# A gated block without Strassen: split operands and three single-pass products, attention first

## The chip, the core and the metric

The kernel runs on one core of a Trainium2 chip. The core has five engines with instruction queues of their own: TensorE (matmuls; PE in the profile, its weight loads PEld), VectorE (DVE), ScalarE (ACT), GpSimd (POOL) and SyncE (SP). Here POOL and SP mostly issue DMA transfers. Matmul results go to PSUM, eight banks of 128 partitions x 512 float32. The metric is the device time of one execution, in microseconds (us); lower is better.

## The reference

Two blocks, one after the other. The attention has 4 batches of 8 heads, 768 tokens and 64 dimensions; a token sees only tokens whose 6-bit hash equals its own. The gated block maps 3072 tokens of 512 values through two weight matrices of 512 x 1536, a silu and a third matrix.

```python
q_bits = (np.einsum('bhsd,dk->bhsk', q, proj) > 0)      # the same for k; 6 bits make a bucket
mask = q_bucket[:, :, :, None] == k_bucket[:, :, None, :]
scores = np.where(mask, scale * np.matmul(q, k.transpose(0, 1, 3, 2)), -1e9)
attn = np.exp(scores - scores.max(-1, keepdims=True))
attn_out = np.matmul(attn / attn.sum(-1, keepdims=True), v)
x = attn_out.transpose(0, 2, 1, 3).reshape(B * S, H * D)
g = x @ w_gate
out = (g * (1 / (1 + np.exp(-g))) * (x @ w_val)) @ w_out
```

The weights arrive as 64-bit floats, so the kernel has to make 32-bit ones of them itself.

## The kernel before

**Attention.** The work goes by pairs of heads, 4 pairs for each of the 4 batches, 16 in all. A pair has two halves (384 query tokens), a half has six units (128 key tokens). `score` (L484) makes the scores of a unit: one float32 matmul per head, and one bf16 matmul on the hash bits that pushes unequal buckets far down; ScalarE takes the exponential into a tile `A`. `attend` (L500) multiplies by v into a bank that collects six units. `add` (L518) sums the exponentials over the units on VectorE, one operation of 128x768 a unit. `total` (L529) sums over partitions with a matmul by ones and takes a reciprocal on VectorE (L548, 384 columns wide); `norm` (L558) applies it. `front` (L388) prepares the next pair: for the first pairs TensorE transposes q and k, and from pair 5 on VectorE does (L457, two operations a pair); then hash matmuls (L412), signs on ScalarE (L417), and spreading of the bits (L426 on VectorE, L429 as a DMA on SP's queue).

**Weights.** `prepare` (L354) is a generator whose steps are handed out along the program. `narrow` (L304) makes float32 of a piece of 128x512 with two ScalarE operations (L297, L298) and three VectorE ones (L311, L313, L316). `form` (L329) makes the sums that the Strassen form needs, and stores blocks in DRAM (`ram`), from where `bring` (L322) fetches them again for each batch with POOL's queue into `room`.

**Gated block.** All products are float32 matmuls, issued at L593 by `product`. `up_strassen` (L599) computes both up products of a batch with seven half-size products in place of eight (Strassen, Winograd's form), and in batches 1 to 3 two of the seven are split once more in the same way (`deeper`, L703, 192 columns). `down_strassen` (L763) does the same with the down product (256 columns). The additions of the form run on VectorE (`plus`, L596), the gate is a tanh on ScalarE (L570) and two VectorE operations.

**Order.** The order of the instructions on each engine is that of the Python text. The main loop (L862) goes over half-pairs. The gated block of a batch is cut into atoms, and once the first batch's attention is done (from half-pair 9 on, `LATE`, L478), each turn issues one half-pair of attention and then atoms up to a credit. So attention of one batch and gated block of the batch before stand side by side through most of the span.

## Time and profile before

| | |
|---|---|
| time, median of 3 runs | 985.93 us (985.88 to 986.16) |
| span of the profiled execution | 983.9 us |
| profiled execution, with the 2.0 us around its span (taken from the median) | 985.9 us |
| TensorE busy | 977.7 us, 4813 matmul records |
| VectorE busy | 669.6 us |
| ScalarE busy | 408.2 us |
| GpSimd busy | 127.2 us |
| moved by DMA | 107.02 MB, mean 109 GB/s |

The span runs from the first to the last instruction. A program's float32 matmul leaves two matmul records, each with a weight load. A record is longer than the time until the next record starts, since matmuls are pipelined; the pace is read from start to start. In the list of groups a line gives: line of the program, engine, operation, output tile <- input tiles, shape, type and count, then busy time and mean ns, then the idle time before with what ended it. In the timeline a line begins with the start and the length of a run of like instructions. `q0` in the DMA table is POOL's queue, with packets, MB, and the time of its packets as a share of 16 DMA engines' span.

### The profile page before, as it was taken

The numbers are of one execution on the slowest core, as the hardware profiler recorded it, in microseconds if no ns is written. First come the engines' busy times: TensorE is split into PE (matmuls) and PEld (weight loads), VectorE is DVE, ScalarE is ACT, GpSimd is POOL, SyncE is SP. The second block draws the span as 40 slices with busy tenths as digits, with TensorE's granted clock in tenths as the row PEclk, the third lists the DMA queues.
The fourth block names the chain that finished last, engine by engine and source line by source line (L and its number), as shares of the span: only waits on it lengthen the run. The fifth ranks groups of instructions, "written<-read, shape, count | busy, mean of one in ns | idle before, by whom it ended". The sixth has DMA issues, their size and how long they took to land.

```text
span 983.9 us, 13575 instructions
## 1 busy us (share of the span) xinstructions
PE 977.7 (99%) x4813; PEld 624.2 (63%) x4813; DVE 669.6 (68%) x1276; ACT 408.2 (41%) x921; POOL 127.2 (13%) x248
## 2 busy tenths in 40 slices
PE   9999999999999999999999999999999999999998
PEld 4444555555576776556567776666556687666787
DVE  5899888888974647768775465676767444767721
ACT  6999555566413225444342224335443212333200
POOL 3232232241100011101110001110101000121000
PEclk9999999999999999999999999999999999999999
DMA  7787685976303043323432204343122011333000
GB/s 231 219 259 220 153 260 171 242 271 172 110 17 78 17 100 106 86 85 93 109 93 45 66 17 113 93 98 103 58 67 76 22 38 65 107 102 110 18 28 33
DMA packets 119987, 107.02 MB, mean 109 GB/s; under 512 B 90032, under 2 KB 104848, under 8 KB 119920
## 3 DMA queue, kind: packets, MB, share of 16 engines
q0 software_dynamic: 18336, 73.29, 23.0%
q1 hardware_dynamic: 100784, 32.67, 14.2%
q8 instruction: 38, 0.62, 0.3%
q10 hardware_dynamic: 800, 0.20, 0.1%
q14 instruction: 29, 0.24, 0.1%
HBM read 81.79 MB, written 17.30 MB: 101 GB/s over the span
## 4 chain that ended last, share of the span: by engine, by line
PE 95%; DVE 2%; ACT 2%; issue 1%; DVEq 0%; ACTq 0%
PE up L593 42%; PE po L593 22%; PE sc L494 15%; PE av L509 12%; PE sum L540 1%; PE hps L412 1%; PE tps L396 1%; ACT A L497 1%; ACT kb L417 1%; DVE room L368 0%; PE idle L134 0%; DVE acc L527 0%; ACT room L497 0%; DVE hid L575 0%; DVE c L571 0%
## 5 line engine op out<-in xcount | busy, mean ns | idle before, releaser
L593 PE MATMUL up<-xT,room 128*128 128x384 f32 (+1 forms) x732 | 243.0, 465 | 0.0
L593 PEld LDWEIGHTS up<-xT,room 128*128 128x128 f32 x732 | 134.8, 190 | 73.3 <-issue 9.8
L593 PE MATMUL up<-xc,room 128*128 128x384 f32 (+1 forms) x540 | 176.9, 455 | 0.0
L327 POOL DMA_DIRECT2D room<-ram x144 | 77.6, 542 | 671.0 <-PE up L593 654.3
L494 PE MATMUL sc<-qT,kT 64*128 64x384 f32 x768 | 159.5, 493 | 0.0
L527 DVE TENSOR_TENSOR acc<-acc,A 128x768 f32<-128x768 f32 x128 | 122.6, 958 | 15.7 <-ACT A L497 2.9
L597 DVE TENSOR_TENSOR c<-c,up 128x192 f32<-128x192 f32 (+1 forms) x198 | 78.8, 406 | 76.7 <-PE up L593 72.3
L593 PEld LDWEIGHTS up<-xc,room 128*128 128x128 f32 x540 | 99.3, 190 | 43.8 <-DVE c L597 1.1
L570 ACT ACTIVATE th<-c 128x384 f32<-128x384 f32 x90 | 47.0, 522 | 156.4 <-DVE c L571 87.6
L497 ACT ACTIVATE A<-sc 128x384 f32<-128x384 f32 x256 | 104.0, 527 | 0.6 <-PE sc L494 0.5
L815 ACT COPY words<-po 128x256 f32<-128x256 f32 x48 | 17.9, 372 | 198.5 <-PE po L593 179.6
L494 PEld LDWEIGHTS sc<-qT,kT 64*128 64x128 f32 x768 | 66.1, 186 | 53.6 <-issue 41.2
L597 DVE TENSOR_TENSOR hid<-hid,up 128x192 f32<-128x192 f32 (+1 forms) x162 | 67.6, 418 | 42.8 <-PE up L593 41.0
L509 PE MATMUL av<-A,vraw 128*64 128x384 f32 (+1 forms) x512 | 88.2, 486 | 0.0
L597 DVE TENSOR_TENSOR words<-words,po 128x256 f32<-128x256 f32 x36 | 15.1, 420 | 95.8 <-PE po L593 95.8
L679 ACT COPY c<-up 128x384 f32<-128x384 f32 x72 | 34.4, 478 | 81.6 <-PE up L593 81.6
L593 PE MATMUL po<-wo,room 128*128 128x256 f32 x288 | 66.3, 379 | 0.5 <-DVE room L597 0.5
L593 PE MATMUL po<-wo,hid 128*128 128x256 f32 x288 | 66.7, 382 | 0.0
L593 PE MATMUL po<-room,hid 128*128 128x256 f32 x288 | 66.2, 379 | 0.5 <-ACT words L815 0.5
L509 PEld LDWEIGHTS av<-A,vraw 128*64 128x64 f32 x512 | 36.7, 137 | 46.0 <-issue 44.4
L494 PE MATMUL sc<-qb,kb 64*128 64x384 bf16 x384 | 63.2, 323 | 0.5 <-DVE kb L426 0.5
L593 PEld LDWEIGHTS po<-wo,hid 128*128 128x128 f32 x288 | 54.1, 190 | 12.1 <-issue 4.9
(137 smaller groups left out, 1166.1 us busy)
## 6 DMA issues: line engine op xcount, KB each, us to landing
room<-ram POOLq DMA_DIRECT2D x96, 384.0 KB, 3.7
vraw<-in_v_dram SPq DMA_DIRECT2D x16, 384.0 KB, 3.3
ram<-room POOLq DMA_DIRECT2D x12, 512.0 KB, 5.0
room<-ram POOLq DMA_DIRECT2D x48, 128.0 KB, 3.5
out_dram<-words SPq DMA_DIRECT2D x48, 128.0 KB, 1.7
room<-in_moe_w_out_dram POOLq DMA_DIRECT2D x10, 512.0 KB, 6.6
qraw<-in_q_dram SPq DMA_DIRECT2D x48, 96.0 KB, 3.0
hid<-in_moe_w_gate_dram POOLq DMA_DIRECT2D x9, 512.0 KB, 6.9
```

The lines of the kernel that those rows point to most:

```text
L327: nc.gpsimd.dma_start(places[k % 2][:, PARTS[go], :], ram[k % NG][:, PARTS[go], :])
L396: nc.tensor.transpose(ps[:, i * P : (i + 1) * P], raws[name, n][:, half * CH + i, :, :].rearrange("p h d -> p (h d)"), ident)
L412: nc.tensor.matmul(tile_[i * BLOCK : (i + 1) * BLOCK, 0:HQ], hash_w, T[name, n][:, half * HQ : (half + 1) * HQ], start=True, stop=True)
L494: nc.tensor.matmul(sc[h], x["k", n][rows, ks], x["q", n][rows, qs], start=start, stop=not start)
L497: nc.scalar.activation(weights(u)[:, h, 0:HQ], sc[h], AF.Exp, scale=SCALE * (OFF / 2 if n <= NP else 1.0))
L509: nc.tensor.matmul(ps[h * D : (h + 1) * D, 0:width], raws["v", n][:, h, c, :], a[:, h, 0:width], start=c == 0, stop=c == NCH - 1)
L527: nc.vector.tensor_tensor(acc[n, half], acc[n, half], a[:, :, 0:HQ], op=ALU.add)
L570: nc.scalar.activation(th, g, AF.Tanh, scale=0.5)
L593: nc.tensor.matmul(ps, a, x, start=start and i == 0, stop=i == len(pairs_) - 1, skip_group_check=True)
L597: nc.vector.tensor_tensor(o, a, b, op=op)
L679: nc.scalar.copy(tile_of(g, spot), c)
L815: nc.scalar.copy(o, c)
```

## The change

Nearly the whole program is rewritten, though attention keeps its instructions.

- All 16 pairs of attention come first, then the gated blocks of all four batches. Nothing of the gated block stands beside attention, apart from weight preparation (four steps a half-pair, until 25 of 36 pieces are stored; the rest one step an atom in the first gated blocks).
- The operands of the gated block are split in a high and a low part, both rounded to the short float32r type, and the difference of the two. Each product is made of three float32r matmuls: high by high and low by low into one bank, difference by difference into another; 4097 times the first less the second is the product. There is no Strassen form.
- x is split after `norm` (a ScalarE cast and two VectorE operations), stored in DRAM (1.2 MB a pair), and loaded back per batch. A weight piece gets a cast on ScalarE and two VectorE operations beyond the three of before, and is stored with its three parts (786 KB). For every use a tile of a ring of seven is loaded with POOL's queue: 144 loads in the gated blocks.
- The reciprocal of the sums works on 12 columns: the sums are laid out by a DMA over 128 partitions, inverted, and spread again through DRAM.
- The exponential tiles form a ring of eight in place of six. The gate is ScalarE's Silu.

The core of the diff; what is left out of attention is moved and indented, not changed:

```diff
-    def narrow(i):
-        ...
-        nc.vector.tensor_tensor(wi, wi, lo, op=ALU.add)
-    def form(n):
-        ...
+    def prepare():
+        for i in range(NPIECE):
+            load_words(i + 1)
+            if i not in staged:
+                scale(i)
+            ...
+            nc.vector.tensor_tensor(wi, wi, lo, op=ALU.add)
+            nc.scalar.activation(r32(st[:, 0]), w, AF.Copy, scale=TOWARD)
+            load_words(i + 4)
+            yield True
+            nc.vector.tensor_tensor(r32(w), w, st[:, 0], op=ALU.subtract)
+            yield True
+            nc.vector.scalar_tensor_tensor(out=r32(st[:, 2]), in0=w, scalar=-STEP, in1=st[:, 0],
+                                           op0=ALU.mult, op1=ALU.add)
+            nc.gpsimd.dma_start(ram[i].bitcast(FP32), st)
+            progress["kept"] = i + 1
+            yield True
+    def bring(count=1):
+        for _ in range(count):
+            ...
+            while progress["kept"] <= at:
+                next(preparing)
+            held[what, n] = t = ringp.tile([P, 3, PIECE], FP32R, tag="ring", name="ring")
+            nc.gpsimd.dma_start(t.bitcast(FP32), ram[at].bitcast(FP32))
         def total(n):
             ...
-            nc.vector.reciprocal(r, ps[:, 0:HQ])
+            nc.scalar.copy(row, ps[:, 0:HQ])
+            few = att.tile([P, each], FP32, tag="few", name="few")
+            nc.sync.dma_start(few, row.rearrange("(g r) t -> r g t", r=BLOCK)[0])
+            waiting.append(lambda: invert(n, few))
+        def invert(n, few):
+            nc.vector.reciprocal(few, few)
+            nc.sync.dma_start(s, few)
+            ...
+            for h in range(2):
+                nc.sync.dma_start(t[h * D : (h + 1) * D].rearrange("p x t -> p (x t)"),
+                                  flat[h : h + 1].to_broadcast([D, 2 * HQ]))
+            return lambda: norm(n, t)
         def norm(n, t):
             nc.vector.scalar_tensor_tensor(out=x, in0=x, scalar=mean[n], ...)
+            nc.scalar.activation(h, x, AF.Copy, scale=TOWARD / STEP)
+            nc.vector.scalar_tensor_tensor(out=l, in0=h.bitcast(FP32), scalar=-STEP, in1=x,
+                                           op0=ALU.mult, op1=ALU.add)
+            nc.vector.tensor_tensor(d, h.bitcast(FP32), l.bitcast(FP32), op=ALU.subtract)
+            nc.sync.dma_start(kept_x[pairs[n]].bitcast(FP32), p.bitcast(FP32))
-    def up_strassen(x, b, first):
-        ...
-    def down_strassen(out_of, at_once):
-        ...
+    def gated_block(scope):
+        ...
+        pp = scope.enter_context(tc.tile_pool(name="pp", bufs=4, space=PSUM))
+            def first():
+                for half in halves_():
+                    for j in range(NJ):
+                        for v in range(2):
+                            mm(a[:, half, 0:HQ], block(v, j), xparts[b, j][:, v, halves[half]],
+                               j == 0 and v == 0, j == NJ - 1 and v == 1)
+            def second():
+                for half in halves_():
+                    for j in range(NJ):
+                        mm(n_[:, half, 0:HQ], block(2, j), xparts[b, j][:, 2, halves[half]],
+                           j == 0, j == NJ - 1)
+                    def one(what=what, z=z):
+                        ops[what] = up(n, what)
+                        ops[what][0]()
+                        nc.scalar.activation(two(z), ops[what][2], AF.Copy, scale=STEP + 1)
+                    def other(what=what, z=z):
+                        _, second, _, n_ = ops[what]
+                        second()
+                        bring()
+                        nc.vector.tensor_tensor(two(z), two(z), n_, op=ALU.subtract)
+                        if what == "g":
+                            nc.scalar.activation(z, z, AF.Silu)
+                            return
+                        nc.vector.tensor_tensor(val, gate, val, op=ALU.mult)
+                        nc.scalar.activation(h, val, AF.Copy, scale=TOWARD / STEP)
+                        def tail():
+                            nc.vector.scalar_tensor_tensor(out=l, in0=h.bitcast(FP32), scalar=-STEP,
+                                                           in1=val, op0=ALU.mult, op1=ALU.add)
+                            nc.vector.tensor_tensor(d, h.bitcast(FP32), l.bitcast(FP32),
+                                                    op=ALU.subtract)
+                        return tail
+                    def chunk(c=c):
+                        t = two_banks("o")
+                        for j in range(NQ):
+                            for v in range(2):
+                                mm(t[:, 0], hs[j][:, v, cols], ws[j][:, v],
+                                   j == 0 and v == 0, j == NQ - 1 and v == 1)
+                        for j in range(NQ):
+                            mm(t[:, 1], hs[j][:, 2, cols], ws[j][:, 2], j == 0, j == NQ - 1)
+                        if part == 0:
+                            nc.scalar.activation(accs[c], t[:, 0], AF.Copy, scale=STEP + 1)
+                        else:
+                            nc.vector.scalar_tensor_tensor(out=accs[c], in0=t[:, 0],
+                                                           scalar=STEP + 1, in1=accs[c],
+                                                           op0=ALU.mult, op1=ALU.add)
+                        nc.vector.tensor_tensor(accs[c], accs[c], t[:, 1], op=ALU.subtract)
+                        if part == NF // NQ - 1:
+                            nc.sync.dma_start(rows[b][:, c, :], accs[c])
+                        if c == NCH - 1:
+                            bring(NQ)
+        for kind, n in order:
+            ...
+            for atom in atoms_of(kind, n):
+                tail = atom()
+                finish(tails)
+                if tail:
+                    tails.append(tail)
+                prepare_on(1)
+    with ExitStack() as scope:
+        attention(scope)
+    bring(7)
+    with ExitStack() as scope:
+        gated_block(scope)
```

In the new program an up-block (128 columns of the gate and of the value matrix, for one batch) has 48 matmuls of 384 columns, and after every third of them a down group of six chunks follows, nine matmuls of 512 columns each.

## The prediction

> **What bounds the kernel now.** First the busy table and the chain that ended last.
>
> ```profile
> PE 977.7 (99%) x4813; PEld 624.2 (63%) x4813; DVE 669.6 (68%) x1276; ACT 408.2 (41%) x921; POOL 127.2 (13%) x248
> ...
> PE 95%; DVE 2%; ACT 2%; issue 1%; DVEq 0%; ACTq 0%
> PE up L593 42%; PE po L593 22%; PE sc L494 15%; PE av L509 12%; PE sum L540 1%; PE hps L412 1%; PE tps L396 1%; ACT A L497 1%; ACT kb L417 1%; DVE room L368 0%; PE idle L134 0%; DVE acc L527 0%; ACT room L497 0%; DVE hid L575 0%; DVE c L571 0%
> ```
>
> TensorE is the chain nearly everywhere, and 64% of it is the gated block (`up`, `po`). So TensorE work counts one for one, and the other engines only where a stage leaves TensorE too little to hide them. Next the matmuls by shape, for counts, and the timeline of TensorE, for their true pace (a record's mean is longer than its pace, because records overlap).
>
> ```profile
> L593 PE MATMUL up<-xT,room 128*128 128x384 f32 x624 | 219.6, 489 | 0.0
> L494 PE MATMUL sc<-qb,kb 64*128 64x384 bf16 x384 | 63.2, 323 | 0.5 <-DVE kb L426 0.5
> ```
>
> ```profile
> 114.98 7.90 PE L593 MATMUL up<-xc,room 128*128 128x384 f32 x24
> 122.72 2.74 PE L593 MATMUL up<-xT,room 128*128 128x384 f32 x8
> ...
> 500.06 0.49 PE L593 MATMUL up<-xc,words 128*128 128x192 f32 x2
> 500.39 0.49 PE L593 MATMUL up<-xc,room 128*128 128x192 f32 x2
> ...
> 508.05 0.33 PE L494 MATMUL sc<-qb,kb 64*128 64x384 bf16 x2
> 508.21 0.81 PE L494 MATMUL sc<-qT,kT 64*128 64x384 f32 x4
> ...
> 939.17 2.75 PE L593 MATMUL po<-wo,room 128*128 128x256 f32 x12
> 941.76 2.75 PE L593 MATMUL po<-room,hid 128*128 128x256 f32 x12
> ```
>
> Start to start: a 384-column f32 record takes 7.74/24 = 0.323 us, a 192-column one 0.33/2 = 0.163, a 256-column one 2.59/12 = 0.216; a 384-column bf16 matmul takes 0.16 (two heads side by side). An f32 matmul of the program leaves two records, so 384 columns cost 0.646 us, four times the bf16 pass. Every record has its own load of 128 f32 weight columns, and the 192-column rows show that such a load is hidden at a pace of 0.163.
>
> Last, the stages: busy time by window, VectorE's rows, and the DMA.
>
> ```profile
> 40.00:60.00 20.00, 19.91 (x139) 9.11 (x136) 18.34 (x23) 18.23 (x41) 5.05 (x9) 1.00 0.82 265
> 80.00:100.00 20.00, 20.00 (x138) 9.18 (x136) 17.83 (x24) 17.68 (x40) 6.70 (x12) 1.00 0.82 243
> 500.00:600.00 100.00, 100.00 (x514) 72.34 (x513) 56.99 (x108) 27.98 (x69) 2.08 (x5) 1.00 0.23 58
> ```
>
> ```profile
> 59.81 4.15 DVE L527 TENSOR_TENSOR acc<-acc,A 128x768 f32<-128x768 f32 x4
> ```
>
> ```profile
> q0 software_dynamic: 18336, 73.29, 23.0%
> ```
>
> Columns of a window: length, then busy PE, PEld, DVE, ACT, POOL, the granted clock, DMA share, GB/s. In the first 97 us, attention alone with weight preparation, VectorE and ScalarE already have 9 of 10 parts full; later the matmuls of the gated block give them room (57 and 28 of 100).
>
> **The change, part by part.** *Products.* Removed by count and pace: 1056 records of 384 columns (341 us), 504 of 192 (82), 1008 of 256 (218), together 641 us. Added: 4 batches x 12 blocks x 48 = 2304 matmuls of 384 columns, and 16 x 6 x 9 = 864 of 512, all on float32r. No row has a float32r matmul. Bounds: it streams a column like the bf16 row (0.162 us for 384, 0.216 for 512), giving 373 + 187 = 560 us; or like an f32 record, which also reads 4 bytes a column (0.323 and 0.431), giving 744 + 372 = 1116. I take 560: the f32 matmul's 0.646 is just four bf16 passes, as it must be if its four half-by-half products each stream the columns once, and float32r has one product. The trace does not exclude the other, since bytes per ns are equal in both rows (768/162 = 1536/323). So 641 becomes 560, -81 us.
>
> The Trainium skill, "SBUF — State Buffer" (section "A bandwidth-pool intuition that's wrong (but worth ruling out)"), gives TensorE's moving operand about 614 GB/s, 128 lanes of 2 bytes at 2.4 GHz; were that a ceiling in bytes, float32r would go at 0.323 and the sum below would be some 540 us longer. "FP8 and Floating Point Precision" (section "TensorE Precision Notes") says that true FP32 is four passes, which fits the 0.646 against 0.16 and speaks for the shorter sum; no run here shows float32r yet.
>
> *Attention by itself.* Pairs 0 to 3 run alone today too: the ninth half-pair starts at 97.1 us, at 21.8 us a pair. The new code gives them nearly the same work: 97. For the other 12 pairs TensorE needs 12 x (0.81 + 0.67) + 0.75 (sums) + 0.65 (hashes) = 19.2 us a pair; I use 19.4. VectorE, now without the gated block's time to hide in: ten adds at 1.04 (10.3), two transposes of 0.97 (1.9), two key spreads of 0.41 (0.8), three 768-wide operations for norm and split by the 1.01 and 0.96 rows (3.0), a reciprocal of 12 columns in place of 384 (at most 0.3; 2.56 before), and 1.6 weight pieces of five operations (0.42 + 4 x 0.69 and gaps, 5.4): 21.7. VectorE becomes the bound. TensorE cannot run away from it, since the hash matmuls of the next pair wait for VectorE's transpose of q in TensorE's order. I take 22 a pair: 264, less 2 for the last, which prepares no successor. Ends: 19.4 a pair (VectorE hidden after all) gives 330 for the stage; 24, if two round trips to ScalarE a pair cost it 1 us each (a piece's cast sits there behind copies that wait for TensorE), gives 383. Taken 97 + 262 = 359.
>
> *Queues.* New on SP's queue are the store of each pair's split x (1.2 MB), which waits for VectorE, and three small transfers of the reciprocal; behind them stand the spread of the next pair's q bits (48 KB, lands in 1.9) and the loads of q and k. The spread is issued some 9 us before the scores that need it, so VectorE may lag by about 7 us at no cost; beyond that, it is part of the 24 us case. On POOL's queue the store of a prepared piece waits for VectorE with the next weight loads behind it.
>
> *The seam.* The sums of the last pair go through copy 0.5, three transfers of about 2 (the 48 KB transfers land in 1.9), norm 1.0 and cast 0.9 before ScalarE is free, about 9 us; TensorE has work for 7.8 of them (four double banks), but its first weights are asked for only after VectorE's last preparation, behind it on POOL's queue, and 786 KB take about 5 (512 KB land in 5.0). The clock was granted in full throughout the trace, the first matmuls excepted (0.43 us for 512 bf16 columns); a gap may bring that back for a few us. Taken 7, ends 4 and 14.
>
> *Weights by DMA.* Each tile of 786 KB is used for 3.9 us of TensorE: 144 tiles, 113 MB, 201 GB/s, seven tiles in the ring. The first batch (140 us) also carries the last 10.4 pieces (5.4 MB in, 8.2 out) and the next x (4.7): 46.6 MB. POOL's queue moved 73.29 MB in 23.0% of 983.9 us, 324 GB/s while its engines worked; at 300, 46.6 MB take 155 us, 15 longer than TensorE. At 324 it is 4. I take 14. Later batches need 34.6 MB in 140 us, 247 GB/s, below that: no stall, with six tiles ahead. If the 265 of the best window is all there is, the first batch loses 36. The Trainium skill, "DMA: Bandwidth & Descriptors" (section "Specifications"), puts the HBM limit of a core at about 358 GB/s; by it there is no stall and the sum is 14 lower.
>
> *Edits with cover.* ScalarE per up-block: two evacuations, Silu, cast, about 0.85 each by the 384-wide rows doubled less their fixed part, 3.4 of 7.8 us. VectorE: five 768-wide operations, 4.9 of 7.8; a down chunk 1.4 of 1.95. While pieces are left, each of an atom's turns adds 0.64: 7.4 of 7.8 and 2.0 of 1.95, so cover is just gone for the two down groups of that time (under 2 us, inside the 14). One more table load, 1.3, in the seam. Combinations, inner weights and tanh (VectorE) go away with no gain, since TensorE hid them. Output: the last chunk needs two VectorE operations (1.4) and a 256 KB store (about 2): 4 after the last matmul, 3 today.
>
> *Sum.* 359 + 7 + 560 + 14 + 4 = 944, plus 2.0 around the span (985.9 - 983.9, the median of the runs standing for the profiled execution): **946 us**, 4% faster. The same counting puts today's last matmul at 97 + 12 x 19.4 + 641 = 971, measured 980.8; the 10 us are small waits, which I leave out of the new sum, as its gated block is plainer.
>
> **Rivals.** *VectorE does not bind attention* (TensorE's 19.4): 330 in place of 359, 917. For it: today it runs 21.2 of 21.8 us without holding TensorE up. Against: 21.7 is over 19.4.
> *The ring starves.* At 265 GB/s the first batch loses 36, total 968; at 243 it loses 52 and the others 2 each, near 990, and below that the kernel is slower. For it: no 20 us of the trace moved over 265. Against: those carried 256-byte pieces of q and k; the ring has 6 KB runs.
> *float32r streams at an f32 record's pace*: 1116 for 560, and no ring stall with twice the time for it: 946 + 556 - 14 = 1488 us, slower. Place: every matmul of the gated block. It decides from 0.174 us for 384 columns, 7% over the row taken, since 40 us over 560 eat the gain.
>
> **How the numbers follow.** Forecast 0.50 (own range 925 to 965); VectorE hidden 0.12; ring starves 0.18, a third of it slower than now; float32r slow 0.12; the rest, 24 us a pair or a long seam, 0.08, half of it slower. Within 0.2% is what a measurement cannot tell from no change. Faster 0.50 + 0.12 + 0.12 + 0.04, less a little for the edge: 0.76; same 0.02; slower 0.22. The range runs from 905 (hidden VectorE and a free ring) to 1000, leaving out float32r slow and the worst of the ring.
>
> **What would show it.** float32r: records of `a`, `n`, `o` at a start-to-start of 0.162 and 0.216, one per matmul. Attention: a pair every 22 us after the fifth, VectorE over 95% there, TensorE's hash matmuls waiting for VectorE; its end near 359. Seam: one TensorE gap of 4 to 14 us. Ring: TensorE waiting for `ring` only in the first 140 us of the gated block. I am wrong if a 384-column record of `up` is over 0.17, if the ring waits persist, or if attention ends far from 359.

## The result, and the profile after

The changed kernel takes 1070.1 us (median of 4 runs, 1065.68 to 1070.96), against 985.9: 1.0846 times the time before, 95% interval 1.0825 to 1.0867. It is slower by 8.5%; forecast were 946 us and a range of 905 to 1000. The profiled execution took 1065.68 us, its span is 1063.9.

First the busy table of the kernel after, and the chain that ended last.

```profile
PE 968.3 (91%) x5413; PEld 730.0 (69%) x5413; DVE 677.6 (64%) x868; ACT 473.7 (45%) x882; POOL 125.0 (12%) x248
...
PE 66%; DMA 12%; DVE 11%; ACT 5%; issue 4%; SPq 2%; DVEq 0%; POOL 0%; ACTq 0%; POOLq 0%
```

TensorE was 95% of the chain before and is 66% now. DMA, VectorE and ScalarE hold a good quarter of it. The next view says where: busy time by window (columns as before: length, then busy PE, PEld, DVE, ACT, POOL, the granted clock, DMA share, GB/s).

```profile
250.00:300.00 50.00, 40.55 (x244) 17.48 (x242) 37.28 (x50) 30.17 (x68) 2.11 (x4) 0.86 0.63 177
350.00:400.00 50.00, 40.29 (x244) 17.27 (x242) 35.74 (x48) 29.45 (x66) 2.58 (x4) 0.88 0.62 170
...
500.00:600.00 100.00, 100.00 (x537) 94.81 (x536) 74.87 (x104) 39.28 (x57) 19.92 (x37) 1.00 0.79 289
```

In attention (the first two lines) *no* engine is full: TensorE 40 of 50, VectorE 36 to 37, ScalarE 30. The gated block (last line) keeps TensorE full at full clock. So there are two separate stories.

**Attention.** The sums of the last pair start at 432.6 us; forecast for the stage were 359. Taken from the starts of the pairs' sum matmuls in the timeline (pairs counted from 0), pair 1 follows pair 0 after 21.7 us, pair 2 after 24.7, and from there on a pair takes 27 to 28 (one 30.9, the last 22.2). The waits of TensorE and ScalarE between 100 and 433 us (total us, times, longest) and the timeline of VectorE and TensorE at one such wait:

```profile
PE hps L337 <- DVE qT L378: 57.8, 11, 9.1
...
ACT parts L479 <- DVE xT L474: 51.3, 12, 7.9
```

```profile
304.65 4.15 DVE L442 TENSOR_TENSOR acc<-acc,A 128x768 f32<-128x768 f32 x4 [0.18 <-ACT A L413]
308.71 0.97 DVE L378 STREAM_TRANSPOSE kT<-kraw 128x768 f32<-128x768 f32 x1
309.61 0.98 DVE L474 SCALAR_TENSOR_TENSOR xT<-xT,e,r 128x768 f32<-128x768 f32 x1
311.49 0.96 DVE L480 SCALAR_TENSOR_TENSOR parts<-parts,xT 128x768 fp32r<-128x768 f32 x1 [0.91 <-ACT parts L479]
312.49 0.96 DVE L482 TENSOR_TENSOR parts<-parts 128x768 fp32r<-128x768 f32 x1
313.36 0.97 DVE L378 STREAM_TRANSPOSE qT<-qraw 128x768 f32<-128x768 f32 x1
```

```profile
305.38 4.11 PE L424 MATMUL av<-A,vraw 128*64 128x386 f32 x24
314.39 0.85 PE L337 MATMUL hps<-qT,hash 128*32 128x384 f32 x2 [4.89 <-DVE qT L378]
```

This is a loop through all engines. VectorE's adds follow ScalarE's exponentials. Behind the last add stand, in VectorE's order, the k transpose, the norm of an earlier pair, a wait for ScalarE's cast, two split operations, and only then the q transpose (313.36) that TensorE's hash matmuls need. TensorE has 4.1 us of `attend` to do meanwhile and then stands for 4.89. While it stands there are no scores, so no exponentials, so no adds. The chain of work that ended last shows the loop of one pair closed (start us, us, what; the next q transpose starts at 313.36, 27.7 us after this one):

```profile
285.69 0.98 DVE qT L378
...
288.22 7.00 PE sc L410 x36
...
308.71 0.97 DVE kT L378
309.69 0.91 DVE xT L474
310.62 0.85 ACT parts L479
311.49 0.97 DVE parts L480
```

From the end of the k transpose to the start of the q transpose (309.68 to 313.36) 3.7 us of norm, cast and split stand in the loop. The waits of TensorE sum to 5.3 us a pair (57.8/11). The first six units' scores after such a wait also run at a lower clock: 7.0 us, where the same stretch takes 5.05 at full clock (in the light version below). As bookkeeping of TensorE's time, the forecast 19.4, these 5.3 and 2.0 make 26.7; that isn't what each cause is worth by itself.

**The seam.** TensorE's timeline where attention ends:

```profile
432.59 0.85 PE L453 MATMUL sum<-acc,ones 128*32 128x384 f32 x8
442.40 4.57 PE L563 MATMUL a<-x,ring 128*128 128x384 f32 x16 [8.95 <-DMA ring<-ram]
...
461.86 5.03 PE L563 MATMUL a<-x,ring 128*128 128x384 f32 x16 [9.34 <-ACT g L605]
```

Two gaps, 18.3 us together, where 7 were forecast. The second waits for an evacuation (a copy of a result out of PSUM) that stands on ScalarE behind the cast of the last pair's x. That cast waits for the norm, and the norm for the reciprocal's transfers, which the prediction put at about 2 us each: in the chain of work the first takes 14.47 us (434.22) and the second 6.10 (448.96).

**The products.** TensorE's timeline in the gated block:

```profile
712.35 2.93 PE L563 MATMUL a<-x,ring 128*128 128x384 f32 x16
715.13 1.55 PE L563 MATMUL n<-x,ring 128*128 128x384 f32 x8
716.51 12.44 PE L563 MATMUL o<-ring,hid 128*128 128x512 f32 x54
728.79 2.96 PE L563 MATMUL a<-x,ring 128*128 128x384 f32 x16
```

Start to start: 2.78/16 = 0.1738 us, 1.38/8 = 0.1725 (taken together 4.16/24 = 0.1733) for 384 columns, and 12.28/54 = 0.2274 for 512. One record per program matmul, as forecast, but 11 ns over the forecast pace each. 2304 x 0.1733 + 864 x 0.2274 = 596 us, against 560.

**Sum, in the profiled execution.** Attention 433.4, seam 18.3, products 596, waits and lowered clock in the first gated block 12 (4.7 us of waits, the slow rows after the two gaps 3.7, 3.5 not placed), tail 4.4, around the span 1.8: 1066. Against the forecast's 359 + 7 + 560 + 14 + 4 + 2, attention is 74 over, the products 36, the seam 11.

### The profile page after: what moved, and what is told of

It reads as the page before. It is cut to its first block, busy times and chain, and to the rows that moved or that the text cites. A ratio compares the mean times of both kernels' runs of the same rounds, so it can differ in the third digit from the quotient of the medians.

```text
span 1063.9 us, 14458 instructions
## 1 busy us (share of the span) xinstructions
PE 968.3 (91%) x5413; PEld 730.0 (69%) x5413; DVE 677.6 (64%) x868; ACT 473.7 (45%) x882; POOL 125.0 (12%) x248
## 4 chain that ended last, share of the span: by engine, by line
PE 66%; DMA 12%; DVE 11%; ACT 5%; issue 4%; SPq 2%; DVEq 0%; POOL 0%; ACTq 0%; POOLq 0%
PE a L563 23%; PE o L563 19%; PE n L563 11%; PE sc L410 7%; DVE acc L442 4%; DMA r<-sums 4%; PE av L424 3%; ACT A L413 3%; DMA sums<-few 2%; DMA few<-row 2%; PE hps L337 2%; SPq L236 2%; DMA ring<-ram 2%; DVE parts L480 1%; DVE xT L474 1%
## 5 line engine op out<-in xcount | busy, mean ns | idle before, releaser
L563 PE MATMUL a<-x,ring 128*128 128x384 f32 x1536 | 285.8, 337 | 18.3 <-ACT g L605 9.3
L563 PEld LDWEIGHTS a<-x,ring 128*128 128x128 f32 x1536 | 271.6, 190 | 20.4 <-ACT g L605 9.7
L563 PE MATMUL o<-ring,hid 128*128 128x512 f32 x864 | 201.8, 392 | 4.6 <-DMA ring<-ram 2.1
L563 PEld LDWEIGHTS o<-ring,hid 128*128 128x128 f32 x864 | 162.8, 189 | 39.6 <-DMA ring<-ram 2.5
L413 ACT ACTIVATE A<-sc 128x384 f32<-128x384 f32 x384 | 158.1, 503 | 18.7 <-PE sc L410 18.3
L563 PE MATMUL n<-x,ring 128*128 128x384 f32 x768 | 148.6, 334 | 0.0
L563 PEld LDWEIGHTS n<-x,ring 128*128 128x128 f32 x768 | 134.5, 188 | 0.0
L424 PE MATMUL av<-A,vraw 128*64 128x386 f32 (+1 forms) x768 | 131.3, 491 | 0.0
L189 POOL DMA_DIRECT2D ring<-ram x144 | 76.2, 531 | 439.2 <-PE n L563 285.3
L649 DVE TENSOR_TENSOR o<-o 128x512 f32<-128x512 f32 x96 | 66.0, 687 | 21.5 <-ACT o L644 19.0
L337 PE MATMUL hps<-qT,hash 128*32 128x384 f32 x64 | 21.0, 724 | 57.8 <-DVE qT L378 57.8
L153 POOL DMA_DIRECT2D ram<-stage x36 | 19.4, 540 | 459.4 <-issue 137.1
L611 DVE TENSOR_TENSOR g<-g,n 128x768 f32<-128x768 f32 x48 | 45.6, 950 | 36.8 <-PE n L563 36.8
```

The source lines that it names most:

```text
L189: nc.gpsimd.dma_start(t.bitcast(FP32), ram[at].bitcast(FP32))
L337: nc.tensor.matmul(tile_[i * BLOCK : (i + 1) * BLOCK, 0:HQ], hash_w, T[name, n][:, half * HQ : (half + 1) * HQ], start=True, stop=True)
L413: nc.scalar.activation(weights(u)[:, h, 0:HQ], sc[h], AF.Exp, scale=SCALE * (OFF / 2 if n <= NP else 1.0))
L424: nc.tensor.matmul(ps[h * D : (h + 1) * D, 0:width], raws["v", n][:, h, c, :], a[:, h, 0:width], start=c == 0, stop=c == NCH - 1)
L563: nc.tensor.matmul(ps, w, x, start=start, stop=stop)
L611: nc.vector.tensor_tensor(two(z), two(z), n_, op=ALU.subtract)
```

## The experiments

The runs named here are edits of the changed kernel. "Last sums" is the start of the last pair's sum matmul, 432.6 in the changed kernel.

### The q transpose ahead of norm

```diff
-                    prepare_pair(2 if n + 1 <= NP else 1)
+                    prepare_pair(2)
```

> VectorE's transpose of q is issued before the norm and split of an earlier pair, not after them; nothing else changes. Theory 'order': TensorE's hash matmuls wait because the transpose of q stands behind about 4 us of norm and split on VectorE, and each gap also halves the clock for some us; the waits at the hash matmuls (57.8 us) and most of the slow clock go, a late pair takes about 22 us in place of 27.7, and the time falls by 50 to 75 us, to 995 to 1020. Theory 'load' (the prediction's): VectorE has more work than TensorE and the order does not matter; a pair stays at 27 to 28, the time within 8 us of 1070. Theory 'reciprocal': the three transfers of the reciprocal are late; the norm then waits longer at its new place and at most 15 us are gained.

Measured: 1059.21 us (1057.44 to 1061.35), ratio to the kernel before 1.0748 (1.0728 to 1.0769); last sums at 422.3. The waits of TensorE and ScalarE over the whole execution:

```profile
PE sc L410 <- ACT A L413: 41.0, 13, 5.7
...
PE hps L337 <- DVE qT L378: 5.6, 11, 0.8
```

```profile
ACT parts L479 <- DVE xT L474: 90.3, 16, 15.5
```

The wait for the transpose is gone (57.8 to 5.6), and another has taken its place: the scores wait 41.0 us for exponentials, which stand on ScalarE behind the cast L479, which waits for VectorE's norm. Eleven us were gained of the 52, far from the 50 to 75 of the theory 'order', and more than the 8 that 'load' allowed. The theory 'reciprocal' allowed these eleven, but VectorE waits for the reciprocal's transfers only 7.8 us in the changed kernel between 100 and 433 us, in four norms, and 8.7 here (to 395).

### The ring's first loads before the last pair

```diff
+            if half == 0 and n == len(pairs) - 2:
+                bring(7)
...
-    bring(7)
     with ExitStack() as scope:
         gated_block(scope)
```

> The first seven ring tiles are asked for in the last pair but one, in place of after the last preparation. Theory 'late weights': the first gap of the seam (9.0 us for the ring) goes, and as the 5.5 MB no longer stand in the way of the last pair's small transfers (the sums took 14.5 us to land), the second gap (9.3 us, ScalarE behind the last norm) shrinks to under 5; the time falls by 10 to 18 us. Theory 'last norm': ScalarE is what holds the gated block; the first gap goes, the second grows by as much, and the time falls by under 4 us.

Measured: 1064.92 us (2 runs), ratio 1.0799 (1.0778 to 1.0821). TensorE's timeline at the end of attention:

```profile
434.45 1.00 PE L410 MATMUL sc<-qT,kT 64*128 64x384 f32 x1 [9.35 <-ACT A L413]
443.39 0.85 PE L453 MATMUL sum<-acc,ones 128*32 128x384 f32 x8
444.96 3.06 PE L565 MATMUL a<-x,ring 128*128 128x384 f32 x16 [0.72 <-ACT row L456]
461.67 5.22 PE L565 MATMUL a<-x,ring 128*128 128x384 f32 x16 [8.09 <-ACT g L607]
```

The gap for the ring falls from 8.95 to 0.72, but a gap of 9.35 appears in the last pair, and the last sums come 10.8 us later; the second gap is 8.09 in place of 9.34. The time falls by 5 us, between the two theories. Seven loads at once beside the small transfers of the reciprocal are the likely cause (a version with one load a half-pair, below, doesn't have the new gap).

### The products by themselves

```diff
-                            mm(a[:, half, 0:HQ], block(v, j), xparts[b, j][:, v, halves[half]],
...
+                            for part in range(2):
...
+                                nc.tensor.matmul(a[:, half, part * (HQ // 2) : (part + 1) * (HQ // 2)],
...
-                        mm(n_[:, half, 0:HQ], block(2, j), xparts[b, j][:, 2, halves[half]],
...
+                        top = [y.bitcast(BF16).rearrange("p (t w) -> p t w", w=2)[:, :, 1]
...
+                        mm(n_[:, half, 0:HQ], top[0], top[1], j == 0, j == NJ - 1)
```

> Two tests of the 0.173 us that a 384-column float32r matmul takes (0.162 predicted). The high and low products are issued as twice as many matmuls of 192 columns, each with its own load of 128 weight columns. If a matmul costs its columns plus a fixed 13 ns, these take 0.093 each, and the time rises by about 20 to 30 us; if the weight load is the bound, they take 0.17 or more, and the time rises by about 250 us. The difference products read only the upper 16 bits of each word as bf16 (this leaves out their low bits): if the 11 ns come with 4-byte operands, they take 0.162 each and 8 us are gained there; if with any change of weights or bank, they stay at 0.173.

Measured: 1140.59 us, one run. TensorE's timeline:

```profile
703.88 3.86 PE L579 MATMUL a<-x,ring 128*128 128x192 f32 x32
707.58 1.53 PE L563 MATMUL n<-x,ring 128*128 128x384 bf16 x8
708.80 12.57 PE L563 MATMUL o<-ring,hid 128*128 128x512 f32 x54
```

A 192-column float32r matmul costs 3.70/32 = 0.1156 us, two thirds of the 384-column one and not half; neither forecast (0.093, or 0.17 and more) came. The bf16 row costs 1.22/8 = 0.153, against 0.1725 for the same columns in float32r: the surplus goes with the 4-byte operands, weights and moving ones together. (A reading over eight matmuls can be off by the edges of the row: the 384-column bf16 matmuls of the scores take 0.16.) No fixed part plus a price per column fits the three float32r paces: from 192 to 384 columns a matmul grows by 0.30 ns a column, from 384 to 512 by 0.42.

### A narrower weight load

```diff
-    for j in range(NJ):
-        for v in range(2):
-            mm(a[:, half, 0:HQ], block(v, j), ...)
+    for v in range(2):
+        for j in range(NJ):
+            m = 64 if v and j < NJ - 1 else P
+            mm(a[0:m, half, 0:HQ], block(v, j)[:, 0:m], ...)
```

> In the products a, three of eight matmuls take only 64 of the 128 weight columns (half of their output is left out, so the result is not the reference's), four with 128 columns first, then three with 64, then one with 128. If the 11 ns over a bf16 column pace come from weight loads that are not wholly hidden, a row of eight gets shorter by some 3 x 11 = 33 ns (16 matmuls from 2.77 to about 2.70 us). If they belong to the streaming of a 4-byte operand or to a matmul's own start, the row stays at 2.77.

Measured: 1071.06 us, one run. TensorE's weight loads by form between 600 and 1000 us (busy, mean ns), then the timeline:

```profile
L563 PEld LDWEIGHTS a<-x,ring 128*128 128x128 f32 x636 | 113.7, 188 | 6.2
...
L563 PEld LDWEIGHTS a<-x,ring 128*64 128x64 f32 x382 | 51.1, 134 | 9.7
```

```profile
703.31 2.94 PE L563 MATMUL a<-x,ring 128*128 128x384 f32 x16
706.09 1.55 PE L563 MATMUL n<-x,ring 128*128 128x384 f32 x8
```

The narrow loads are shorter (134 against 188 ns), and the row of 16 still takes 2.78 us. So at 384 columns the 11 ns are not a part of the weight load that goes with its width. Whether they are a fixed part of it, the start of a matmul or the reading of 4-byte operands stays open, and so does what holds the 192-column matmul at 0.1156.

### The clock by itself

```diff
             def hash_blocks(todo):
+                if n > NP:
+                    ps = bank("idle")
+                    for _ in range(18):
+                        nc.tensor.matmul(ps, quiet[:, 0:P], quiet, start=True, stop=True)
```

> 18 matmuls on zeros (512 bf16 columns, 3.9 us) are put before the hash matmuls of the pairs from 5 on, into the gap; the order is as in the changed kernel. If the clock that falls after each gap costs 2 us or more a pair (the scores after a gap take 7.0 us, 4.9 otherwise), the pair falls from 27.7 to about 25.5 and the time by 20 to 25 us, the granted clock in the late pairs from 0.86 to about 1. If the clock is only a companion and VectorE sets the pair, the time stays within 5 us.

Measured: 1062.43 us, one run; last sums at 429.5. The window between 250 and 300 us:

```profile
250.00:300.00 50.00, 45.05 (x286) 20.73 (x282) 37.49 (x50) 28.38 (x64) 3.34 (x6) 1.00 0.64 175
```

The granted clock is back at 1.00 and the pairs still take 25 to 31 us (26.9 on average from pair 3 on, 27.2 before). Four late pairs do fall to 25.2 to 25.6, but others take 27 to 31, and the hash matmuls still wait 21.6 us behind the added ones. So in this one run the full clock by itself is worth some 3 us of attention, not the 20 to 25 of the first theory; the low clock is in the main a companion of the waits.

### The wait moved from place to place

Eight versions put the steps of the loop elsewhere, one after the other. Where the norm comes later, one small tile (`mean`) also gets three buffers, a line not shown here.

Norm and split at the end of the first half, after the next loads:

```diff
...
-            if half == 0:
-                finish(last)
-            else:
+            if half:
                 while waiting:
...
+            if half == 0:
+                finish(last)
             prepare_on(4)
```

> Norm and split of an earlier pair are issued at the end of the first half, after the transpose of q, the hash matmuls and their first signs, on all engines; q_first had moved only the transposes. Theory 'in-order cast': with q first, what stops the pair is the cast of the split, which stands in ScalarE's queue ahead of the copies, signs and exponentials of the next half while it waits for VectorE's norm (90 us in 16 waits) and, through it, TensorE's scores wait 41 us for exponentials. At the later place the cast waits under 2 us a pair, TensorE's waits at the scores fall under 15 us, a late pair takes 22 to 24 us, and the time is 1000 to 1025. Theory 'load': VectorE's 21.7 us of work with its gaps is what a pair takes; the time stays within 8 us of the 1059 of q_first. Theory 'reciprocal': the norm still waits for its transfers at the later place, and under 15 us are gained.

Measured: 1061.59 us (2 runs), ratio 1.0768 (1.0747 to 1.079); last sums 427.5. Now the scores wait 49.4 us for exponentials, and ScalarE 64.4 us for a weight piece (L146 behind VectorE's L145).

The q transpose first, and the cast of x on VectorE (0.56 us):

```diff
-            nc.scalar.activation(h, x, AF.Copy, scale=TOWARD / STEP)
+            nc.vector.tensor_single_scalar(h, x, TOWARD / STEP, op=ALU.mult)
```

> As q_first (transposes ahead of the norm), and the cast of the split of x is made by VectorE, which gets 0.5 to 1 us more work a pair. Theory 'in-order cast': ScalarE no longer waits for the norm, so the scores no longer wait for exponentials, and the time falls by 20 to 40 us from 1059 although VectorE works more. Theory 'load': VectorE is the bound, and the time rises by 6 to 15 us.

Measured: 1056.49 us (2 runs), ratio 1.0716 (1.068 to 1.0753); last sums 424.2. The ScalarE wait for norm is gone, that for the weight piece grew (34.8 with the q transpose alone, 48.0 here), and scores still wait 36.8.

Late norm, and one ring load in each of the last seven halves:

```diff
+            if u >= N - 7 * NCH:
+                bring()
...
-    bring(7)
```

> The norm at the late place, and the first seven ring tiles asked for one at a time in the last seven half-pairs, in place of all at once. The early ring alone gave nothing: it removed the first gap of the seam (9.0 us to 0.7), but a wait of 9.4 us for exponentials appeared in the last pair, whose norm came late as 5.5 MB went by. Theory 'in-order cast and shared DMA': spread out and with ScalarE free, the first gap stays under 2 us and nothing comes in its place in attention; 8 to 15 us less than the late norm alone. Theory 'last norm': the seam's second gap (8 to 9 us, ScalarE behind the last norm) grows by what the first loses; under 4 us less.

Measured: 1051.98 us (1051.1 to 1052.78), ratio 1.067 (1.0654 to 1.0686); last sums 427.8, and the first gap of the seam 0.73. That is 9.6 us less than with late norm alone: spread loads keep what seven at once had given back. The second gap is 8.45.

The same with the cast of x on VectorE:

> Late norm, spread ring, and the cast of the split of x on VectorE. Theory 'in-order cast': at the late place little is left to gain in the pairs, within 5 us of the run before; in the seam ScalarE is free to empty the first products while the last norm waits for its transfers, so the second gap falls under 6 us, if VectorE, which does wait there in order, is not what then stops it. Theory 'load': 6 to 15 us slower than the run before.

Measured: 1043.02 us (1041.17 to 1044.78), ratio 1.0578 (1.0561 to 1.0596); last sums 420.6. The second gap of the seam was to fall under 6 us and stays at 8.69; it now waits for VectorE, which stands behind the last norm. The waits that are left, on TensorE and on ScalarE:

```profile
PE sc L410 <- ACT A L413: 40.1, 11, 6.7
```

```profile
ACT stage L146 <- DVE stage L145: 68.2, 23, 7.6
```

The same with the weight piece's cast on VectorE too (0.43 us):

```diff
-            nc.scalar.activation(r32(st[:, 0]), w, AF.Copy, scale=TOWARD)
+            nc.vector.tensor_single_scalar(r32(st[:, 0]), w, TOWARD, op=ALU.mult)
```

> The run before this (late norm, spread ring, split of x cast by VectorE) with the cast of the weight pieces moved to VectorE as well, 0.4 us more for it on each of 1.6 pieces a pair. In attention ScalarE then never waits for a result of VectorE in front of its exponentials. Theory 'in-order cast': what is left over in the slow pairs (27 to 31 us beside 22) is ScalarE waiting for a piece's sum ahead of the exponentials (68 us in 23 waits), with TensorE's scores behind it (40 us); these go, nearly all late pairs take 22 to 23, the last sums of attention are made near 375 in place of 420.6, and the time is 990 to 1005. Theory 'load': VectorE has 1 us more a pair, the time rises from 1043 by 8 to 12.

Measured: 1035.14 us (2 runs), ratio 1.0499 (1.0478 to 1.052); last sums 407.7. Both ScalarE waits are gone with the casts. Scores now wait 29.8 us for VectorE: the profile names the reciprocal L462, which stands directly behind the spread of the key bits (L351) that the scores need, and the second half's adds stand ahead of both.

Casts back on ScalarE, but a whole piece a half-pair, its cast issued only after the next half's exponentials (with late norm and spread ring loads):

```diff
-            nc.scalar.activation(r32(st[:, 0]), w, AF.Copy, scale=TOWARD)
+            casts.append(lambda: nc.scalar.activation(r32(st[:, 0]), w, AF.Copy, scale=TOWARD))
             load_words(i + 4)
-            yield True
+            yield False
+            finish(casts)
...
             finish(rest)
+            finish(casts)
```

> Both casts stay on ScalarE. Preparation goes piece by piece, one a half-pair, and the cast of a piece is put behind the exponentials of the next half, when VectorE has long made what it reads; norm late, ring spread. VectorE prepares 2 pieces a pair in place of 1.6, 1.3 us more. Theory 'in-order cast': ScalarE waits little for VectorE ahead of exponentials; late pairs take 23 to 24, the time is 995 to 1015. Theory 'load': over 1050.

Measured: 1043.42 us (2 runs), ratio 1.0583 (1.056 to 1.0606); last sums 412.6.

The same with norm and split at the end of the second half:

```diff
             if half:
+                ready = last[:]
+                last.clear()
                 while waiting:
...
-            if half == 0:
-                finish(last)
+            if half:
+                finish(ready)
             prepare_piece()
```

> As the deferred casts, with norm and split of an earlier pair one half later, at the end of the second half, where VectorE has no transposes and the reciprocal's transfers have 10 us more. If the norm's transfers still hold VectorE in half 1's place (waits of 1.8 us and more for them) and the transposes crowd it, a pair gains 1 to 2 us more, late pairs 22 to 23, time 980 to 1000. If not, within 8 us of the deferred casts alone.

Measured: 1032.74 us (1031.54 to 1033.47), ratio 1.0473 (1.0458 to 1.0489); last sums 405.4.

And with the cast of x on VectorE:

> As the last, with the cast of the split of x on VectorE (0.56 us a pair more there). If ScalarE's wait for the norm is the last one ahead of exponentials, 5 to 15 us less than without; if VectorE is now full, 5 to 10 us more.

Measured: 1027.71 us (1025.16 to 1028.36), ratio 1.0417 (1.04 to 1.0435), the best that still does all the work; last sums 398.7, pairs 24.8 and 26.3 by turns. A window and the main wait of this version:

```profile
250.00:300.00 50.00, 43.38 (x268) 18.90 (x266) 42.10 (x58) 32.98 (x75) 5.17 (x8) 0.90 0.72 217
```

```profile
PE hps L343 <- DVE qT L384: 34.3, 11, 3.8
```

VectorE is now at 42 of 50, and every pair's hash matmuls wait about 3 us for its transpose. These eight versions differ in the length and the place of the wait, and in nothing that removes work. Only two brought a gain that a theory had forecast: the spread loads (9.6, forecast 8 to 15 us) and the last one (5.0, forecast 5 to 15). The others that had forecast a time by order (here, and the q transpose alone above) missed it by 17 to 39 us, as another wait took the place of the one removed; 'load' had the late norm alone right (1061.6 beside 1059), and nowhere else. What these versions can't tell is how much of the 25 us is load.

### Load against order

Two runs take the weight work away from late pairs, one with the changed kernel's order, one with the order just shown (called mended below; it also has the cast of x on VectorE, the spread ring loads, and two whole weight pieces a pair in place of 1.6).

```diff
-    NPIECE = len(pieces)
+    NPIECE = 12
...
-            at = place[what, n % NF]
+            at = place[what, n % NF] % NPIECE
```

> The changed kernel, but only the first 12 weight pieces are prepared (the other 24 are left out, and the ring loads the 12 again in their place, so the result of the gated blocks is not the reference's). From about pair 8 on VectorE has no weight work: 21.7 - 5.4 = about 16.3 us of work a pair, well under TensorE's 19.4. Theory A (the order of waits sets the pair: the q transpose stands behind norm and the wait for ScalarE's cast, and that cast stands in ScalarE ahead of the exponentials): late pairs stay at 23 to 26 us, and the waits of the hash matmuls for VectorE's transpose stay. Theory B (VectorE's load sets the pair): late pairs fall to 19.4 to 20, and attention ends some 50 us earlier than in the changed kernel.

> The last version of the reordered attention (norm and split at the end of the second half, cast of x on VectorE, spread ring loads), again with only 12 weight pieces prepared and loaded again, 24 left out (the result of the gated blocks is not the reference's). Its pairs were 24.7 to 26.3 us with the weight work in. Theory A: without it nothing stands ahead of the transposes, and late pairs go to 19.4 to 21 us, while the run above with the old order stays over 23. Theory B: both runs come to 19.4 to 20. If this run stays at 23 or more, a third cause, neither VectorE's work nor these waits, holds the pairs.

Measured, old order: 1051.8 us (2 runs), ratio 1.0668 (1.0618 to 1.0717). A window and TensorE's waits between 200 and 400 us:

```profile
300.00:350.00 50.00, 41.58 (x260) 17.85 (x258) 30.26 (x36) 26.19 (x61) 0.00 (x0) 0.91 0.39 102
```

```profile
PE hps L337 <- DVE qT L378: 41.1, 7, 15.7
```

VectorE has only 30 of 50 parts to do, and the pairs from 9 to 13 take 26.8, 27.1, 27.2, 27.2, 27.3 us, as with the whole load (pair 8 took 37.9, with the one wait of 15.7, in which VectorE waits 7.5 for a late load of k and 3.8 for the transfers of a reciprocal). The removed work stood where VectorE was waiting anyway.

Measured, mended order: 987.95 us (8 runs, 983.76 to 989.32), ratio 1.0008 (0.999 to 1.0025). The same view between 250 and 300, and TensorE's waits from 227 to 348:

```profile
250.00:300.00 50.00, 48.73 (x334) 21.70 (x332) 36.96 (x45) 32.10 (x78) 0.00 (x0) 1.00 0.56 149
```

```profile
PE hps L343 <- DVE qT L384: 2.5, 6, 0.4
```

Every pair from 8 to 14 takes 20.4 us, at full clock. In the chain of work the q transpose now follows the k transpose at once, and the scores run at 5.05 us:

```profile
274.93 0.97 DVE kT L384
275.90 0.87 DVE qT L384
...
277.67 5.05 PE sc L416 x36
```

Both runs came out as theory A had it, but order isn't all: with the weight work the same order takes 25.5. By windows over five or six whole pairs, VectorE's work is 19.8 us a pair in the changed kernel (246.76 to 410.37) and 15.1 in its light version (254.67 to 390.24), 21.5 in the mended order (202.60 to 355.80) and 15.5 in its light version (227.24 to 349.72). With the order as changed, 4.7 us less work a pair are worth nothing (27.2 with it and without). With the order mended, 6.0 us less are worth 5.1 (25.5 against 20.4). The order alone is worth 1.7 us a pair (while VectorE has 1.7 more to do), the load alone none, both together 6.8.

The light runs also take away ScalarE's operations on these pieces and their transfers. That it is VectorE's part which costs the 5.1 us is argued from the trace of the mended order with the whole load: five operations on pieces (305.96 to 309.19) stand on VectorE without a gap ahead of the adds and the two transposes, and the hash matmuls behind these wait 3.18 us.

## Why the prediction was wrong

**"VectorE becomes the bound", "I take 22 a pair".** This is the step that failed, with 74 us. VectorE's work was not sized too low. In the window from 250 to 300 us it is busy 37.28 of 50 (75%, where the prediction's own sign was over 95%), 20.3 us for a pair of 27.2, under the 21.7 forecast. That the hash matmuls would wait for VectorE's q transpose was right. What failed is the step from a sum of durations to a period: a pair takes what its loop takes, and in the loop VectorE's and TensorE's times stand partly one after the other. The upper end (383, "24 if two round trips to ScalarE a pair cost it 1 us each") priced a round trip by what VectorE loses, 0.91 us at L480. What counts is what TensorE loses behind the whole row of norm, cast and split that stands ahead of the q transpose, 5.3 us a pair and the clock after it. The paragraph on queues allowed VectorE "to lag by about 7 us at no cost", counting from the transfer of q's bits; the q transpose feeds the hash matmuls directly and has no such slack. Before, the atoms of the gated block stood between in TensorE's order from the second batch on; the prediction named that cover for VectorE's load and not for its latency. That they hid this loop is argued from the order, no run shows it.

The statement that pairs 0 to 3 keep their 97 us also failed: their last sums, which stand 1.8 us behind the start of the ninth half-pair, come at 106.6. With the mended order they come at 99.3 (100.2 while the cast of x was still on ScalarE), so again it is order; the light versions still make their pieces there and say nothing on load.

**Products, 560.** The mechanism was right; the term was mis-sized by 36 us. Right were one record a matmul and a pace far under that of an f32 record. The rows measured are 0.1733 and 0.2274 in place of 0.162 and 0.216. The prediction gave 0.174 as the point at which the gain is gone, and the pace fell on it. The light version shows this: attention ends at 368 there, 9 us after the forecast, and the kernel still ties with the one before.

The ceiling that the Trainium skill's page "SBUF — State Buffer" (section "A bandwidth-pool intuition that's wrong (but worth ruling out)") invites, 614 GB/s for the moving operand (given there for bf16), is not one in bytes: 128 lanes of 1536 bytes in 0.1733 us are 1134 GB/s. Its alternative for the sum, some 540 us more, did not come.

**Seam, 7.** Measured 18.3. The first gap (8.95) is the one described, ended by the ring; the second (9.34) was not foreseen, an evacuation on ScalarE behind the cast of the last x. Spread loads take the first away. It is also gone (0.60) in the light version with the old order, whose last pieces don't hold POOL's queue up; that speaks for the prediction's account of it. In every version that removes it and prepares all weights, a gap of 8 to 14 us remains; in the light versions it is 5.1 (old order) and 8.95 (mended).

**Ring, 14, and the rival that it starves.** Neither came. In the gated block TensorE waits for `ring` 8.95 us at the seam and 2.1 us after it. That the measured sum has 12 us in the place of these 14 is luck: the rest of it is the clock after the two gaps, other waits and what could not be placed. The cap of 300 GB/s was too low, as the windows at the start of the gated block show:

```profile
440.00:450.00 10.00, 7.60 (x35) 7.63 (x36) 1.11 (x2) 0.15 (x1) 0.53 (x1) 0.71 1.02 399
450.00:500.00 50.00, 38.60 (x191) 36.17 (x190) 33.75 (x43) 22.21 (x32) 7.76 (x13) 0.86 0.90 357
```

The Trainium skill, "DMA: Bandwidth & Descriptors" (section "Specifications"), gives about 358 GB/s for a core's HBM limit. Over 50 us the trace reads the same (357); over 10 us it reads 399, more than the page's figure. A share of 1.02, over one, shows that in so short a window the view is off by a few per cent, but not by the 11 that lie between. By the page no stall was due, and but for the 2.1 us that was right.

**Tail, 4.** Right (4.4). **VectorE hidden, 917:** the rival's 19.4 is near what a pair takes once nothing waits, 20.4, but only without the weight work. Its argument that VectorE "runs 21.2 of 21.8 us" today reads high: in the kernel before it is busy 20.0 us from 40.0 to 61.8 and 19.8 from 61.8 to 83.6. **float32r at an f32 record's pace, 1488:** did not come.

No version run here beats the kernel before. With products of 596 us, attention, seam and tail would have to fit in 390; the light version takes 392 for these and leaves out two thirds of the weight preparation.

## What to carry to other kernels

When work that filled TensorE's order is moved away from a stage, don't price the stage by its fullest engine. Follow one period around the loop, in each engine's order, from the last add to the next matmul that needs it, and count what stands in between, waits for other engines included. And where a whole change rests on the pace of one instruction that no row shows, a few per cent on it can be the whole gain: price the point of balance first.

## What the runs showed of the hardware

- A float32r matmul with 128 x 128 weights costs 0.1156 us for 192 columns, 0.1733 for 384 and 0.2274 for 512, against 0.153 to 0.16 for 384 columns in bf16. Loads of 64 weight columns in place of 128 (134 ns against 188) for three matmuls in eight change nothing at 384 columns.
- With gaps of 4 to 5 us in each pair the granted clock is 0.83 to 0.88 in the four 50-us windows from 200 to 400 us. With 18 bf16 matmuls (3.9 us) in the gap it is 1.00 from 250 to 300, and attention gains only about 3 us.
- Seven loads of 786 KB started together stand beside a slow small one: the 6 KB layout of the last sums takes 14.47 us in the chain of work (434.22 to 448.69), against 4.82 us for the same transfer in the chain of a middle pair. That the seven loads are the cause isn't shown by itself. One load each half-pair didn't hold the pairs up (last sums 427.8 against 427.5 without).
